# K and V with 32 adjacent keys of two kv-heads per partition, and staging in one tile

## The chip, the cores and the metric

The kernel runs on one core of a Trainium2 chip. The metric is the time of the device in microseconds for one execution; before the change it is 284.9 us, the median of three runs (283.17 to 286.01). A core has a matrix engine (PE, with its weight loads as PEld), a vector engine (DVE), a scalar engine (ACT), GpSimd (POOL) and SyncE (SP). ACT, SP and POOL issue transfers; all transfers run on the core's 16 DMA engines.

## The reference

A decode step of a block with attention over a sliding window and a gated FFN in parallel, forward and backward:

```python
def _A_ref(x, k_cache, v_cache, wq, wo):
    B, Sq, D = x.shape                    # 4, 1, 512
    Hq, Dh = 32, 128
    Hkv, Sk = k_cache.shape[1], k_cache.shape[2]   # 8, 4096
    W = min(4096, max(256, Sk // 4))      # 1024
    rep = Hq // Hkv
    q = (lambda x, *d: x.transpose(*d))((x @ wq).reshape(B, Sq, Hq, Dh), 0, 2, 1, 3)
    k = jnp.repeat(k_cache[:, :, Sk - W:, :], rep, axis=1)
    v = jnp.repeat(v_cache[:, :, Sk - W:, :], rep, axis=1)
    scores = jnp.einsum("bhqd,bhkd->bhqk", q, k) * (Dh ** -0.5)
    p = _softmax(scores, axis=-1)
    o = jnp.einsum("bhqk,bhkd->bhqd", p, v)
    return (lambda x, *d: x.transpose(*d))(o, 0, 2, 1, 3).reshape(B, Sq, Hq * Dh) @ wo
def _B_ref(x, w_gate, w_up, w_down):
    return (_gelu(x @ w_gate) * (x @ w_up)) @ w_down
xn = _layernorm(x, axis=-1)
return x + _A_ref(xn, ...) + _B_ref(xn, ...)
```

The results are this output and the gradients with respect to x, both caches and the five weights, all in bf16. The gradients of the caches have the full shape (4, 8, 4096, 128); outside the window of 1024 keys they are zero, so three quarters of each is a store of zeros.

## The kernel before, in words

There are B = 4 batches, G = 8 kv-heads with rep = 4 query heads each (Q = 32 query heads), J = 8, and the 128 partitions are used as four quadrants of 32 (`quad`).

The FFN comes first. Its weights, then wq, wo and the first K go out on SP's queue; the FFN's weight gradients are evicted from PSUM into staging tiles (`stg_tile`, line 101) and stored by `result` (line 112) on POOL's queue. The staging tiles are [128, 4096] bf16, 8 KB per partition, in rotation over four buffers.

The attention runs over the batches. `load_kv` (line 216) loads K (tiles ka and kb in turn) or V (tile va) of a batch as two transfers of 1 MB, each four kv-heads. Partition m holds 8 adjacent keys (m*8 to m*8+7) of all 8 heads, so a row of a transfer is 8 keys of one head, 2 KB. The DRAM side is written `"g (m j) d -> m g (j d)"`: 128 partitions outermost, then four heads. V of batch b+1 is loaded after the output matmuls of batch b, K of batch b+2 after the dq matmuls of batch b, all but the first K on POOL's queue.

`scores` (line 471) turns the tile with four DVE transposes of 32x32 blocks of bf16 pairs (`t32`), and multiplies with the block-diagonal query tiles bd, which `refill` (line 462) builds on POOL by eight copies per operand and batch. PE's column group c is here the head pair c, and the rows of a quadrant are four key chunks times 8 query heads. `softmax` (509) and `softmax_d` (536) work on [128, 256]. `turned` (496) transposes P or dS through PE into pT and evicts it with one cast of 256 columns. `odq` (567) multiplies pT with V or K. `spread` (487) and `dvdk` (550) form the gradients of V and K: 8 groups of PE results, evicted by `evac` (line 82, it chooses ACT or DVE by a running account of their load) into two staging tiles, which go out as two stores of 1 MB with rows of 2 KB.

The zeros are stores of 1.5 MB from one tile ztile, issued on SP's queue by `zeros` (line 236). Each waits for the zero store two (late in the kernel three) before it, and for an instruction that the caller names: after the loads the first of a group waits until that load has landed. The instruction order of SP's queue is written by hand; the other engines' is the scheduler's, in which the loads of K and V have high priority.

The weight gradients dwo and dwq end the kernel: eight stores of 1 MB with rows of 8 KB, on POOL's queue.

Of the kernel before, what the change touches and what calls it, by code (L numbers as in the profile page):

```python
# [9 lines left out]
ALU = mybir.AluOpType  # L10
AX = mybir.AxisListType
FP32 = mybir.dt.float32
BF16 = mybir.dt.bfloat16
# [5 lines left out]
def kernel(  # L19
# [54 lines left out]
    stage = ctx.enter_context(tc.tile_pool(name="stage", bufs=4, reuse_waits="tile"))  # L74
# [26 lines left out]
    def stg_tile():  # L101
        return stage.tile([P, 4096], BF16, name="stg", tag="stg")
# [46 lines left out]
    def mask(name, n, in_):  # L149
        t_ = const.tile([P, n], FP32, name=name)  # L150
        nc.vector.reduce_sum(out=t_[:], in_=in_, axis=AX.X)
        return t_
# [7 lines left out]
    omt = const.tile([P, NQ, 2], FP32, name="omt")  # L160
    TT(out=omt[:], in0=gmask[:].rearrange("p (c g) -> p c g", g=2), in1=bm[:].unsqueeze(2).broadcast_to([P, NQ, 2]),
       op=ALU.mult)
    om = mask("om", 2, omt[:].rearrange("p c g -> p g c"))
    oms = const.tile([P, 2], FP32, name="oms")
    TS(out=oms[:], in0=om[:], scalar1=scale, scalar2=None, op0=ALU.mult)
    gmask_b = const.tile([P, G], BF16, name="gmask_b")
    nc.vector.tensor_copy(out=gmask_b[:], in_=gmask[:])
    rs2 = const.tile([P, NQ, 4, 8], FP32, name="rs2")
    for c in range(NQ):
        TS(out=rs2[:, c], in0=m8[:].unsqueeze(1).broadcast_to([P, 4, 8]), scalar1=bm[:, c:c + 1], scalar2=None,  # L170
           op0=ALU.mult)
    rs2_f = rs2[:].rearrange("p c a r -> p (c a r)")
    selp = const.tile([P, 4, NQ, 8], BF16, name="selp")
    for a in range(4):
        TS(out=selp[:, a], in0=rs2[:, :, 0, :], scalar1=amask[:, a:a + 1], scalar2=None, op0=ALU.mult)
# [40 lines left out]
    def load_kv(b, k, pool, tag, eng, **kw):  # L216
        d_, src = ((k_t, A_k_cache), (v_t, A_v_cache))[k]
        tl = pool.tile([P, G, J, Dh], BF16, name=tag, tag=tag)
        for hf in range(2):
            hs = slice(hf * G // 2, (hf + 1) * G // 2)  # L220
            with tc.high_priority():
                d = eng.dma_start(out=tl[:, hs].rearrange("p g j d -> p g (j d)"),  # L222
                                  in_=src[b, hs, K0:Sk, :].rearrange("g (m j) d -> m g (j d)", j=J), **kw)
        d_[b] = tl
        return d
# [149 lines left out]
    with tc.tile_pool(name="mid", bufs=1, reuse_waits="tile") as mid:  # L375
# [4 lines left out]
        with tc.tile_pool(name="att", bufs=1, reuse_waits="tile") as att:  # L380
# [7 lines left out]
            for k in range(2):  # L388
                bd.append([])
                for u in range(2):  # L390
                    t_ = att.tile([P, DPB, NQ, 2, 2, Q], BF16, name=f"bd{k}{u}")
                    nc.gpsimd.memset(t_[:], 0.0)
                    bd[k].append(t_)
# [8 lines left out]
            for h in range(Hq):  # L402
                for c in range(C):
# [3 lines left out]
            qs2 = qsc[:, 512:1024].rearrange("p (b c a r) -> p b c a r", b=B, c=NQ, a=4)  # L407
            nc.scalar.activation(out=qs, in_=q_ps[:].rearrange("p h b -> p b h").unsqueeze(2).broadcast_to([P, B, NQ, Hq]),
                                 func=ACT.Copy, scale=scale)
            nc.vector.tensor_copy(out=qs2, in_=qs[:, :, 0, :].rearrange("p b (c r) -> p b c r", c=NQ).unsqueeze(3)  # L410
                                  .broadcast_to([P, B, NQ, 4, 8]))

            def spread_rows(k, get):

                ps = bank("r_ps", "x", (P, B, Dh))
                get(ps, 0)
                rb = scratch()[:].bitcast(BF16)[:, 0:512]
                nc.scalar.copy(out=rb, in_=ps[:].rearrange("p b d -> p (b d)"))
                t32(D3[k][:], pairs(rb), 256)
                ps = bank("r_ps", "x", (P, B, Dh))  # L420
                get(ps, 1)
                nc.scalar.activation(out=rows[k][:, :, 0, :], in_=ps[:], func=ACT.Copy, scale=g2m[:, 0:1])
                TS(out=rows[k][:, :, 1, :], in0=ps[:], scalar1=g2m[:, 1:2], scalar2=None, op0=ALU.mult)

            def get_q(ps, u):
                for b in range(B):
                    l_ = qs[:, b].rearrange("p a h -> p (a h)") if u == 0 else qs2[:, b].rearrange("p c a r -> p (c a r)")
                    mm(ps[:, b, :], l_, ident[:])
# [13 lines left out]
            for u in range(2):  # L442
# [5 lines left out]
            hsel2 = dsc[:, 640:768].rearrange("p (c a r) -> p c a r", c=NQ, a=4)  # L448
            nc.vector.tensor_copy(out=hsel, in_=hm[:].unsqueeze(1).broadcast_to([P, NQ, Q]))
            nc.vector.tensor_copy(out=hsel2, in_=hm[:].rearrange("p (c r) -> p c r", c=NQ).unsqueeze(2)  # L450
                                  .broadcast_to([P, NQ, 4, 8]))
# [4 lines left out]
            def get_d(ps, u):  # L456
                l_ = dsc[:, 512:640] if u == 0 else dsc[:, 640:768]
                mm(ps[:].rearrange("p b d -> p (b d)"), l_, dM.rearrange("p b e k -> p (b e k)"))
# [3 lines left out]
            def refill(k, b):  # L462

                src = D3[k][:].bitcast(BF16).rearrange("p b e (c g i r) -> p b g e c r i", c=NQ, g=2, r=2)
                t_ = bd[k][b % 2]
                for a, q in enumerate(quad):
                    for g2 in range(2):
                        o_ = a * 8 + g2 * 4
                        nc.gpsimd.tensor_copy(out=t_[q, :, :, g2, :, o_:o_ + 4], in_=src[q, b, g2])

            def scores(k, b):

                t_ = bd[k][b % 2]
                ps = bank("sc_ps", ("S", "dP")[k], (P, NJ))
                src = pairs((k_t, v_t)[k][b][:])
                for g2 in range(2):
                    for e in range(2):
                        sc = scratch()
                        t32(sc[:].rearrange("p (c j m) -> p c j m", c=NQ, j=J), src[:, g2:G:2, :, e * Q:(e + 1) * Q], 1024)
                        sb = sc[:].bitcast(BF16).rearrange("p (c n r) -> p c r n", c=NQ, r=2)  # L480
                        for r in range(2):
                            for c, q in enumerate(quad):
                                mm(ps[q, :], t_[:, e, c, g2, r, :], sb[:, c, r, :], g2 == 0 and e == 0 and r == 0,
                                   g2 == 1 and e == 1 and r == 1, (0, Q * c))
                return ps[:]
# [10 lines left out]
            def turned(src, k):  # L496

                ps = bank("pT_ps", "x", (P, J, Q))
                for j in range(J):
                    for a, q in enumerate(quad):  # L500
                        mm(ps[q, j, :], src[:, j * Q:(j + 1) * Q], selp[:, a].rearrange("p c r -> p (c r)"), pos=(0, Q * a))
                pT = att.tile([P, J, Q], BF16, name="pT", tag=f"pT{k}")
                evac(pT[:], ps[:], NJ)
                return pT
# [4 lines left out]
            def softmax(S):  # L509
# [4 lines left out]
                mx = small("mx", (1, NQ, 8))  # L514
                nc.vector.reduce_max(out=mx[:], in_=mT_ps[:].rearrange("o (c a r) -> o c r a", c=NQ, a=4), axis=AX.X)
                mx4 = small("mx4", (1, NQ, 4, 8))
                TS(out=mx4[:], in0=mx[:].unsqueeze(2).broadcast_to([1, NQ, 4, 8]), scalar1=-1.0, scalar2=None, op0=ALU.mult)
                nm_ps = bank("nm_ps", "x", (P, 1))
                mm(nm_ps[:], mx4[:].rearrange("o c a r -> o (c a r)"), one_f[:])
# [6 lines left out]
                mm(es_ps[:], rs2_f, es[:])  # L526
# [9 lines left out]
            def softmax_d(P_f, dP):  # L536
# [5 lines left out]
                mm(gs_ps[:], rs2_f, gs[:])  # L542
# [7 lines left out]
            def dvdk(k, b, sp, r_):  # L550

                og = (out_3, out_2)[k]
                stg = [stg_tile() for _ in range(2)]
                sv = [s_[:].rearrange("p (g j d) -> p j g d", g=4, j=J) for s_ in stg]
                for j in range(0, J, 2):
                    ps = [bank("kv_ps", "w", (P, 2, 2, Dh)) for _ in range(NQ)]
                    for u in range(2):
                        for c, q in enumerate(quad):
                            mm(ps[c][:, u].rearrange("p g d -> p (g d)"), sp[q, j + u].rearrange("p a m -> p (a m)"),
                               r_[q, b].rearrange("p g d -> p (g d)"), pos=(Q * c, 0))  # L560
                    for c in range(NQ):
                        evac(sv[c // 2][:, j:j + 2, (c % 2) * 2:(c % 2) * 2 + 2, :], ps[c][:], 512)
                for hf in range(2):
                    result(og[b, hf * 4:(hf + 1) * 4, K0:Sk, :].rearrange("g (m j) d -> m g (j d)", j=J),
                           stg[hf][:].rearrange("p (g e) -> p g e", g=4))

            def odq(k, b, pT):
# [3 lines left out]
                for j in range(J):  # L571
                    for c, q in enumerate(quad):
                        mm(ps[q].rearrange("p g d -> p (g d)"), pT[:, j, :], src[:, 2 * c:2 * c + 2, j, :],
                           j == 0, j == J - 1, (0, Q * c))
                mk = (om, oms)[k]
# [190 lines left out]
```

## Time and profile before

| | |
|---|---|
| median of three runs | 284.9 us |
| the profiled execution | 284.82 us |
| its span | 283.0 us |
| PE, DVE, ACT, POOL busy | 66%, 58%, 44%, 21% |
| moved | 112.21 MB, 396 GB/s over the span |
| SP's queue (q1) and POOL's queue (q0), share of 16 DMA engines | 57.0% and 40.8% |
| transfers of 1 MB for K and V | 16 loads, 16 stores |
| zero stores | 32 of 1.5 MB |

The span is the time from the first to the last instruction that the profiler saw; the execution's time has about 1.8 us more around it. A DMA packet is one contiguous piece that one of the 16 DMA engines moves; the share of a queue is the time of its packets over the span of 16 engines. Releasers are written with an arrow: "A <- B" is A waiting for B.

### The profile page before, as it was taken

How to read it: one execution, taken by the hardware profiler on the slowest of the kernel's cores; microseconds unless marked ns; L12 is line 12 of the kernel's file. 1: busy time of each engine (PE TensorE's matmuls, PEld its weight loads, DVE VectorE, ACT ScalarE, POOL GpSimd, SP SyncE). 2: the span in 40 equal slices, each digit the busy share in tenths (PEclk: the TensorE clock that was granted, in tenths of full speed). 3: DMA queues.
4: the chain of work that ended last, by engine and by line, in shares of the span. 5: the costliest groups of instructions: out<-in, count | busy, mean ns of one | idle time of the engine just before them, and what ended most of it. 6: DMA issues, size and time to landing. Idle time of an engine off the chain costs nothing.

```text
span 283.0 us, 4400 instructions
## 1 busy us (share of the span) xinstructions
PE 187.6 (66%) x1731; PEld 76.8 (27%) x1733; DVE 165.0 (58%) x309; ACT 124.4 (44%) x245; POOL 60.3 (21%) x135
## 2 busy tenths in 40 slices
PE   0225989859544899759976663923357998944870
PEld 0102344233111543234331341311034232510210
DVE  4779674898798533635257254055496104396970
ACT  2032774740010469744725420802432767454870
POOL 8500000169075313120040060200020020201110
PEclk9999965556955555755555555555555555685555
DMA  6999989999999999999999999999999999999995
GB/s 217 430 446 435 432 317 420 424 430 396 392 428 406 383 357 425 328 365 411 421 419 414 408 427 405 396 422 421 429 382 423 413 410 403 399 415 396 391 397 223
DMA packets 16883, 112.21 MB, mean 396 GB/s; under 512 B 1368, under 2 KB 1632, under 8 KB 11104
## 3 DMA queue, kind: packets, MB, share of 16 engines
q1 hardware_dynamic: 6544, 66.46, 57.0%
q0 software_dynamic: 10176, 45.35, 40.8%
q8 instruction: 13, 0.21, 0.3%
q10 hardware_dynamic: 144, 0.13, 0.2%
q14 instruction: 6, 0.05, 0.0%
HBM read 30.93 MB, written 81.01 MB: 396 GB/s over the span
## 4 chain that ended last, share of the span: by engine, by line
DMA 30%; issue 14%; PE 13%; DVE 9%; ACT 3%; POOL 2%; POOLq 0%; ACTq 0%; DVEq 0%
DMA out_dram<-stg 30%; DVE scr L93 4%; PE kv_ps L117 4%; PE od_ps L117 3%; PE sc_ps L117 2%; PE dwq_ps L117 2%; ACT stg L88 2%; DVE stg L89 1%; POOL out_dram L106 1%; PE ok_ps L117 1%; PE es_ps L117 1%; DVE spr L492 1%; DVE dqs L593 1%; ACT E_f L524 1%; PE nm_ps L117 1%
## 5 line engine op out<-in xcount | busy, mean ns | idle before, releaser
L88 ACT CAST stg<-kv_ps 128x512 bf16<-128x512 f32 x118 | 63.6, 606 | 52.2 <-DMA out_dram<-stg 26.3
L106 POOL DMA_DIRECT2D out_dram<-stg x30 | 19.7, 659 | 150.0 <-ACT stg L88 94.7
L117 PE MATMUL sc_ps<-scr,bd 128*32 128x256 bf16 x256 | 24.2, 396 | 15.2 <-DVE scr L93 15.2
L117 PE MATMUL kv_ps<-qm,spr 32*128 32x256 bf16 x128 | 24.8, 385 | 13.0 <-ACT stg L88 12.5
L117 PE MATMUL kv_ps<-dm,spr 32*128 32x256 bf16 x128 | 28.9, 399 | 6.6 <-ACT stg L88 4.9
L93 DVE STREAM_TRANSPOSE scr<-va 128x1024 uint32<-128x1024 uint32 x16 | 18.9, 1219 | 12.9 <-DMA va<-in_A_v_cache_dram 12.8
L117 PEld LDWEIGHTS <-spr 32*128 32x128 bf16 x256 | 12.4, 102 | 46.4 <-issue 42.1
L89 DVE CAST stg<-kv_ps 128x512 bf16<-128x512 f32 x10 | 6.6, 683 | 17.0 <-PE kv_ps L117 11.0
L117 PEld LDWEIGHTS <-bd 128*32 128x32 bf16 x256 | 8.1, 107 | 29.1 <-issue 28.5
L88 ACT CAST stg<-dwg_ps 128x448 bf16<-128x448 f32 x26 | 12.7, 554 | 6.4 <-PE dwg_ps L117 5.5
L88 ACT CAST stg<-dwo_ps 128x512 bf16<-128x512 f32 x18 | 10.0, 588 | 11.4 <-PE dwo_ps L117 10.1
L117 PE MATMUL dwo_ps<-dy_b,oSP 32*128 32x512 bf16 x32 | 9.0, 508 | 7.5 <-ACT stg L88 6.2
L93 DVE STREAM_TRANSPOSE scr<-ka 128x1024 uint32<-128x1024 uint32 x8 | 9.6, 1228 | 5.2 <-DMA ka<-in_A_k_cache_dram 3.1
L222 POOL DMA_DIRECT2D va<-in_A_v_cache_dram x8 | 6.0, 757 | 27.3 <-PE od_ps L117 25.8
L93 DVE STREAM_TRANSPOSE scr<-kb 128x1024 uint32<-128x1024 uint32 x8 | 9.8, 1232 | 3.5 <-DMA kb<-in_A_k_cache_dram 2.9
L117 PE MATMUL do_ps<-scr,dyBD 128*128 128x512 bf16 x31 | 10.1, 459 | 2.4 <-DVE scr L93 2.1
L578 DVE SCALAR_TENSOR_TENSOR odt<-od_ps,oms,odt 128x128 f32<-128x128 f32 x4 | 1.4, 340 | 17.0 <-ACT odt L577 17.0
L117 PE MATMUL dwq_ps<-dqSP,xn_b 32*128 32x512 bf16 x32 | 10.7, 586 | 0.9 <-ACT stg L88 0.3
L89 DVE CAST stg<-dwq_ps 128x512 bf16<-128x512 f32 x15 | 9.9, 689 | 1.6 <-PE dwq_ps L117 1.4
L89 DVE CAST stg<-dwo_ps 128x512 bf16<-128x512 f32 x14 | 9.2, 680 | 2.7 <-PE dwo_ps L117 2.7
L117 PEld LDWEIGHTS <-pT 128*32 128x32 bf16 x256 | 9.2, 140 | 5.2 <-ACT pT L88 2.3
L88 ACT CAST stg<-dwq_ps 128x512 bf16<-128x512 f32 x17 | 9.7, 586 | 1.4 <-PE dwq_ps L117 0.7
(196 smaller groups left out, 321.3 us busy)
## 6 DMA issues: line engine op xcount, KB each, us to landing
out_dram<-ztile SPq DMA_DIRECT2D x32, 1536.0 KB, 12.1
out_dram<-stg POOLq DMA_DIRECT2D x24, 1024.0 KB, 13.7
va<-in_A_v_cache_dram POOLq DMA_DIRECT2D x8, 1024.0 KB, 17.6
out_dram<-stg POOLq DMA_DIRECT2D x6, 896.0 KB, 10.2
wq_sb<-in_A_wq_dram SPq DMA_DIRECT2D x1, 4096.0 KB, 25.6
wo_sb<-in_A_wo_dram SPq DMA_DIRECT2D x1, 4096.0 KB, 36.7
kb<-in_A_k_cache_dram POOLq DMA_DIRECT2D x4, 1024.0 KB, 19.4
ka<-in_A_k_cache_dram SPq DMA_DIRECT2D x2, 1024.0 KB, 44.3
```

The lines of the kernel that those rows point to most:

```text
L88: return nc.scalar.copy(out=out, in_=in_)
L89: return nc.vector.tensor_copy(out=out, in_=in_)
L93: nc.vector.transpose(out=out, in_=in_)
L106: d = eng.dma_start(out=out, in_=in_, **kw)
L117: nc.tensor.matmul(out, lhsT=lhsT, rhs=rhs, start=first, stop=last, **kw)
L222: d = eng.dma_start(out=tl[:, hs].rearrange("p g j d -> p g (j d)"), in_=src[b, hs, K0:Sk, :].rearrange("g (m j) d -> m g (j d)", j=J), **kw)
L492: TS(out=sp[:, :, a, :], in0=src[:].rearrange("p (j m) -> p j m", j=J), scalar1=amask[:, a:a + 1], scalar2=None, op0=ALU.mult)
L524: nc.scalar.activation(out=E_f[:], in_=S, func=ACT.Exp, bias=negm[:, 0:1], scale=1.0, accum_out=es[:])
L578: done = STT(out=t_[:], in0=ps[:, 1, :], scalar=mk[:, 1:2], in1=t_[:], op0=ALU.mult, op1=ALU.add)
L593: nc.vector.tensor_copy(out=dqs[q, :, :, :, a * B + b], in_=d3v[q])
```

## The change

K and V are laid out anew. A partition now holds 32 adjacent keys of two kv-heads: quadrant q holds the head pair q (heads 2q and 2q+1), and partition m in it the keys m*32 to m*32+31. A transfer is one head of each pair (g2), so a row is 32 keys of one head, 8 KB; the DRAM side is `"q (m j) d -> q m (j d)"`. On PE the column groups are now the key quarters, and rows of a quadrant are all 32 query heads. So the masks, the block-diagonal tiles (`refill` is now two products with a mask instead of eight copies, and the memsets go), the order of heads in the softmax and the sums over partitions change with it; one form of the rows (`spread_rows`) serves where there were two. `turned` masks pT to its head pair while it evicts it: the cast of 256 columns on ACT or DVE becomes a DVE product of 1024 columns. The four staging tiles become one tile of four slots, because an eviction of `dvdk` now writes into both of its slots; `stg_tile(2)` gives an aligned pair.

```diff
-    stage = ctx.enter_context(tc.tile_pool(name="stage", bufs=4, reuse_waits="tile"))
+    stage = ctx.enter_context(tc.tile_pool(name="stage", bufs=1))
...
-    def stg_tile():
-        return stage.tile([P, 4096], BF16, name="stg", tag="stg")
+    stg_all = stage.tile([P, 4, 4096], BF16, name="stg")
+    stg_next = [0]
+
+    def stg_tile(n=1):
+
+        k = stg_next[0] = -(-stg_next[0] // n) * n
+        stg_next[0] += n
+        return stg_all[:, k % 4] if n == 1 else stg_all[:, k % 4:k % 4 + n]
...
-    rs2 = const.tile([P, NQ, 4, 8], FP32, name="rs2")
-    for c in range(NQ):
-        TS(out=rs2[:, c], in0=m8[:].unsqueeze(1).broadcast_to([P, 4, 8]), scalar1=bm[:, c:c + 1], scalar2=None,
-           op0=ALU.mult)
-    rs2_f = rs2[:].rearrange("p c a r -> p (c a r)")
-    selp = const.tile([P, 4, NQ, 8], BF16, name="selp")
-    for a in range(4):
-        TS(out=selp[:, a], in0=rs2[:, :, 0, :], scalar1=amask[:, a:a + 1], scalar2=None, op0=ALU.mult)
+    selp = const.tile([P, NQ, 4, 8], BF16, name="selp")
+    for c in range(4):
+        for a in range(NQ):
+            TS(out=selp[:, c, a, :], in0=m8[:], scalar1=amask[:, c:c + 1], scalar2=bm[:, a:a + 1], op0=ALU.mult,
+               op1=ALU.mult)
...
-        tl = pool.tile([P, G, J, Dh], BF16, name=tag, tag=tag)
-        for hf in range(2):
-            hs = slice(hf * G // 2, (hf + 1) * G // 2)
+        tl = pool.tile([P, 2, Q, Dh], BF16, name=tag, tag=tag)
+        for g2 in range(2):
             with tc.high_priority():
-                d = eng.dma_start(out=tl[:, hs].rearrange("p g j d -> p g (j d)"),
-                                  in_=src[b, hs, K0:Sk, :].rearrange("g (m j) d -> m g (j d)", j=J), **kw)
+                d = eng.dma_start(out=tl[:, g2].rearrange("p j d -> p (j d)"),
+                                  in_=src[b, g2::2, K0:Sk, :].rearrange("q (m j) d -> q m (j d)", j=Q), **kw)
...
-                t_ = bd[k][b % 2]
-                for a, q in enumerate(quad):
-                    for g2 in range(2):
-                        o_ = a * 8 + g2 * 4
-                        nc.gpsimd.tensor_copy(out=t_[q, :, :, g2, :, o_:o_ + 4], in_=src[q, b, g2])
+                for g2 in range(2):
+                    nc.gpsimd.tensor_tensor(out=bd[k][b % 2][:, g2], in0=src[:, b],
+                                            in1=hmask[:, g2].unsqueeze(1).unsqueeze(1).broadcast_to([P, DPB, 2, Q]),
+                                            op=ALU.mult)
...
-                pT = att.tile([P, J, Q], BF16, name="pT", tag=f"pT{k}")
-                evac(pT[:], ps[:], NJ)
+                load["dve"] += 1200
+                pT = att.tile([P, J, NQ, NQ, 8], BF16, name="pT", tag=f"pT{k}")
+                TT(out=pT[:].rearrange("p j a c r -> p (j a) c r"),
+                   in0=ps[:].rearrange("p j (a r) -> p (j a) r", a=NQ).unsqueeze(2).broadcast_to([P, J * NQ, NQ, 8]),
+                   in1=bm[:].unsqueeze(1).unsqueeze(3).broadcast_to([P, J * NQ, NQ, 8]), op=ALU.mult)
...
-                stg = [stg_tile() for _ in range(2)]
-                sv = [s_[:].rearrange("p (g j d) -> p j g d", g=4, j=J) for s_ in stg]
+                stg = stg_tile(2)
+                sv = stg.rearrange("p g (j d) -> p j g d", j=Q)
...
-                    for c in range(NQ):
-                        evac(sv[c // 2][:, j:j + 2, (c % 2) * 2:(c % 2) * 2 + 2, :], ps[c][:], 512)
-                for hf in range(2):
-                    result(og[b, hf * 4:(hf + 1) * 4, K0:Sk, :].rearrange("g (m j) d -> m g (j d)", j=J),
-                           stg[hf][:].rearrange("p (g e) -> p g e", g=4))
+                    for a in range(NQ):
+                        evac(sv[:, J * a + j:J * a + j + 2], ps[a][:], 512)
+                for g2 in range(2):
+                    result(og[b, g2::2, K0:Sk, :].rearrange("q (m j) d -> q m (j d)", j=Q), stg[:, g2])
```

## The prediction

> **What bounds the kernel now.** I read first the engines' shares, the forty slices, the DMA queues and the DMA issues of the page.
>
> ```profile
> span 283.0 us, 4400 instructions
> ...
> PE 187.6 (66%) x1731; PEld 76.8 (27%) x1733; DVE 165.0 (58%) x309; ACT 124.4 (44%) x245; POOL 60.3 (21%) x135
> ...
> DMA  6999989999999999999999999999999999999995
> ...
> DMA packets 16883, 112.21 MB, mean 396 GB/s; under 512 B 1368, under 2 KB 1632, under 8 KB 11104
> ...
> q1 hardware_dynamic: 6544, 66.46, 57.0%
> q0 software_dynamic: 10176, 45.35, 40.8%
> ...
> out_dram<-ztile SPq DMA_DIRECT2D x32, 1536.0 KB, 12.1
> out_dram<-stg POOLq DMA_DIRECT2D x24, 1024.0 KB, 13.7
> va<-in_A_v_cache_dram POOLq DMA_DIRECT2D x8, 1024.0 KB, 17.6
> ```
>
> No compute engine is above 66%, while the 16 DMA engines are full in nearly every slice. The two large queues fill 57.0 + 40.8 = 97.8% of 16 engines' span, 276.8 of 283.0 us; about 5 us (first load, last landing) are not theirs. So the kernel is a DMA schedule: what a change does to the packets is worth its full price, and what it does to an engine is worth nothing while that engine keeps the queues fed. The sum below is made on the profiled execution (284.82 us, 1.8 above its span), which agrees with the median of the three runs, 284.9. Their spread (283.17 to 286.01) means that a difference under about 1% can't be told from none.
>
> Next, what the queues wait for (SP's waits) and when POOL issues (timeline of POOL).
>
> ```profile
> SPq L106 <- DMA out_dram<-ztile: 127.1, 21, 14.5
> ...
> SPq L106 <- DMA va<-in_A_v_cache_dram: 23.2, 4, 9.2
> SPq L106 <- DMA ka<-in_A_k_cache_dram: 13.3, 1, 13.3
> ```
>
> ```profile
> 162.63 1.50 POOL L222 DMA_DIRECT2D va<-in_A_v_cache_dram  x2 [16.20 <-PE od_ps L117]
> 164.12 1.50 POOL L106 DMA_DIRECT2D out_dram<-stg  x2
> ...
> 182.12 1.50 POOL L106 DMA_DIRECT2D out_dram<-stg  x2 [14.66 <-ACT stg L88]
> 206.23 0.75 POOL L106 DMA_DIRECT2D out_dram<-stg  x1 [22.61 <-DVE stg L89]
> 207.48 0.75 POOL L106 DMA_DIRECT2D out_dram<-stg  x1 [0.50 <-ACT stg L88]
> 228.84 0.75 POOL L106 DMA_DIRECT2D out_dram<-stg  x1 [20.61 <-ACT stg L88]
> ```
>
> The zero stores (SP's queue) are the filler: they wait for the zero store two or three before them and, in groups, for a load to land. A zero store is complete only when its slowest DMA engine is. So if some DMA engines fall behind, the zeros are held back for all of them.
>
> **The change, part by part.** (1) *Longer rows.* K and V are 16 MB loaded and 16 MB stored, 32 transfers of 1 MB (16 loads, 16 stores; 30 on POOL's queue, two on SP's). In the trace's packet records POOL's 30 are 7680 packets of 4096 B, mean 169.4 ns, SP's two 1024 packets of 2048 B, mean 85.4 ns. Now all have rows of 8 KB, as the dwo and dwq stores have: 1024 packets of 8192 B, mean 318.2 ns. The DMA time per engine, if spread over all 16: before (7680 x 169.4 + 1024 x 85.4) / 16 = 86.8 us, after 4096 x 318.2 / 16 = 81.5 us, a gain of 5.3 us. With the medians (160, 84, 315 ns) it is only 1.5 us: the long packets are hardly faster per byte, and the mean of the short ones contains crowded stretches.
>
> (2) *How many DMA engines carry one transfer.* Before, the DRAM side ran over m (128) first, then the heads; both sides of each K/V transfer counted 128. Now the DRAM side is "q m (j d)": 4 head pairs outermost, 32 rows in each, against 128 partitions in SBUF. No large transfer of before has a 4 outermost. The nearest rows are the two small result stores (out_b, dx_b), four rows each. The 1368 packets under 512 B show how they are spread: there are 85 large or 128-partition transfers (44 by POOL, 40 by SP, 1 by ACT) and these two, and 85 x 16 + 2 x 4 = 1368. These tiny packets are one per participating engine, so a transfer with 4 outermost took four engines. The ends for the new transfers are therefore 16 (their SBUF side still counts 128) and 4; I take 4, from the only rows with that outer count. Then one 1 MB transfer is 32 packets of 8 KB on each of four engines, 32 x 318.2 ns = 10.2 us, and leaves twelve engines to others. What matters is how the 32 transfers fall on the engines. SP's two (the first K) come from the queue that sent the small stores; I put both on the same four: 20.4 us there. POOL's 30 can't be dealt evenly to four groups: 8, 8, 7, 7 if taken in turn. The ends are wide, for the trace does not show which engines a transfer takes: dealt perfectly nothing is lost, and all on one group would be 30 x 10.2 + 20.4 = 326 us there, a time of 284.8 - 86.8 + 326 = 524. I take turns, by the row above: POOL's 44 transfers all took every engine alike, so nothing marks four of them out for it, and I give the far end no more than 2 in 100. With turns the fullest group carries 8 x 10.2 + 20.4 = 101.9 us against 86.8 before: **+15.1 us**. If that group gets seven, +4.9 us.
>
> [...]
>
> (3) *What the concentration does to the others.* The load and store pairs alternate on POOL (va and stores at 162.6 and 164.1), and a pair fills eight engines, so mostly a load pair on one half stands beside a store pair on the other. Where a pair has no partner (stores at 182.1 and 228.8), the half without it runs ahead and waits for the zeros to complete: at most the pair's own 10.2 us each. At 182 the loads of 162.6 are still being worked off on the other half, so I take nothing; at 228.8 the next pair follows 12 us later, and I take half, **+5.1 us**. Bounds 0 and 20.4.
>
> (4) *One staging tile.* Each eviction now writes both stores' slots, so a first eviction waits for both earlier stores instead of one; the second is issued 0.75 us after the first (1.50 for two), 8 x 0.75 = 6 us of ACT waiting at most. Behind the waiting ACT stand its exp and odt work and, through the four PSUM banks, PE's kv_ps matmuls. The gap from slot 9 to 10 is a free slot. Cover: the zeros and loads in flight; taken as 0.
>
> (5) *The turned P and dS.* ACT's cast pT 128x256 (402 ns) becomes a DVE product of 1024 columns. Between DVE's 128x512 from PSUM (L423, 0.71 us) and twice that: 1.42 us at most, so up to +1.0 us x 8 = 8 us in the batches' serial chains, and -0.40 x 8 on ACT. Off the DMA queues: 0; if that cover is gone, up to 8.
>
> (6) *Small edits.* Refills: 64 POOL copies of 229 ns become 16 products of 128 columns (POOL's nearest row is 0.97 us for 1024, so 0.1 to 0.5 each): some 7 us less POOL; four bd memsets (0.97 each) fall away. Second row spread: 4 + 1 matmuls (307 to 460 ns) and two DVE copies fewer, some 2 us between 68 and 80 us. Masks: sixteen selp products at 236 ns for four, less four rs2 at 299 and three small ones, +1.4 us of DVE before xn_b; the weights that follow land later than that. Scores, odq and dvdk keep their counts and shapes. All stand beside full DMA queues: 0. POOL's issue order stays, an issue of 128 rows took 0.53 us against 0.75: 0.
>
> Sum: 284.8 + 15.1 + 5.1 = **305.0 us**.
>
> **The rivals.** *All sixteen engines* (the other side, faster): if POOL spreads by partitions, part 2 falls away and only part 1 stays: 284.8 - 5.3 = 279.5, or 283.3 by medians. For it: every POOL transfer so far has 16 participants and SBUF still counts 128. Against: the 4 is outermost now, as in the two small stores. It decides as soon as a 1 MB load alone on the queues lands in far less than 10 us.
> *Collapse of the cover* (slower): the zeros are gated by five later load pairs (SP waited 23.2 + 13.3 us on such loads already). If each leaves eight engines idle for half of its 10.2 us, 25.5 us, and both lone store pairs cost their full 10.2, with part 5's 8 us uncovered: 284.8 + 15.1 + 20.4 + 25.5 + 8 = 353.8, and all above 328 is this case. One staging tile that serializes its halves would end there too: a store landing (13.7) on each of seven gradient pairs, +96 at most. Against: before, load and store pairs overlapped.
> *Even enough* (no large effect): the group with SP's loads gets seven, and longer rows and quicker landings on free engines offset the rest: 283 to 291.
>
> **How the numbers follow.** Four engines with the fullest group as the bound 0.62: its own range 290 (seven shares, no idling: 284.8 + 4.9) to 328 (both lone pairs in full, part 5 uncovered: 284.8 + 15.1 + 20.4 + 8). All sixteen 0.17, collapse 0.11, even enough 0.10. The range reaches into the first rival, 280 to 328. Faster by over 1%: most of the first rival, 0.15; within 1%: the rest of it and half of "even enough", 0.08; slower 0.77.
>
> **What would show it.** Right: packets of 8192 B on both queues; the count under 512 B falls by 2 x 12 on SP's queue; the DMA row of the slices shows 7 and 8 where it had 9; a K or V load takes at least 10.2 us; SP waits longer for zeros. Wrong: DMA row full to the end and a shorter span (sixteen engines), or DMA clearly idle while ACT and PE wait for stg (the staging tile).

## The result, and the profile after

The changed kernel takes 407.2 us (median of four, 403.99 to 410.08) against 284.4 us before: 1.43 times as long, 95% interval 1.412 to 1.443. The direction was forecast; the size was not, and the time lies far above the range of 280 to 328. Here and below a median and the range beside it hold all runs of a kernel, while a ratio to before, with its interval, leaves out runs that took over 1.5% longer than the kernel's fastest.

The parts of the changed kernel's page that answer to those shown of before:

```profile
span 402.2 us, 4365 instructions
...
PE 189.5 (47%) x1728; PEld 73.3 (18%) x1728; DVE 169.8 (42%) x314; ACT 126.5 (31%) x247; POOL 48.4 (12%) x83
...
DMA  7999958998599799999999589979999689999577
GB/s 273 438 441 370 419 229 201 152 186 302 219 429 309 186 143 194 312 317 261 294 319 350 184 266 256 331 234 254 222 238 330 263 224 293 268 283 358 213 309 292
DMA packets 23772, 112.26 MB, mean 279 GB/s; under 512 B 12865, under 2 KB 13129, under 8 KB 13897
...
q0 software_dynamic: 17856, 45.40, 45.9%
q1 hardware_dynamic: 5752, 66.46, 42.4%
...
out_dram<-ztile SPq DMA_DIRECT2D x32, 1536.0 KB, 18.4
out_dram<-stg POOLq DMA_DIRECT2D x24, 1024.0 KB, 35.0
va<-in_A_v_cache_dram POOLq DMA_DIRECT2D x8, 1024.0 KB, 34.2
```

The engines are hardly busier than before (PE 187.6 us then and 189.5 now, DVE 165.0 and 169.8), so the 119 us of span are waiting, and the transfers come first in question. Two things must be read together. The DMA row has holes (5, 6, 7 and 8 where there were nines). And where it is full, the GB/s row beneath it is not: 152 or 143 GB/s under a 9. A stretch of the kernel before with full queues moved 367 GB/s (stretch, length, busy time of PE, PEld, DVE, ACT and POOL, granted PE clock, DMA share, GB/s):

```profile
97.00:125.00 28.00, 24.05 (x256) 10.85 (x255) 11.52 (x29) 19.74 (x41) 6.17 (x11) 0.56 0.99 367
```

The same view of the changed kernel shows few engines at work from 56 to 60 us, full but slow ones from 138 to 152, and a hole from 224 to 230:

```profile
56.00:60.00 4.00, 3.85 (x26) 0.98 (x23) 2.27 (x7) 4.00 (x10) 0.53 (x1) 0.50 0.29 120
...
138.00:152.00 14.00, 0.00 (x0) 0.00 (x0) 0.00 (x0) 0.00 (x0) 0.00 (x0) 0.50 1.03 143
224.00:230.00 6.00, 1.12 (x8) 0.34 (x7) 0.00 (x0) 1.76 (x4) 0.00 (x0) 0.50 0.42 150
```

From 138 to 152 us all 16 DMA engines are at work on four loads (V issued at 121.6 us, K at 134.9) and two stores of the changed form and move 143 GB/s, while no compute engine does anything. The 8 KB packets that start there take 937 ns on average: a busy DMA engine is here one whose packet takes about three times the 318 ns of the weight-gradient stores before. From 56 to 60 us between four and five engines are busy (0.29 of 16), by the packet records about half of them with SP's two first K loads and half with the end of a weight-gradient store. The waits say who paid; before:

```profile
ACT stg L88 <- DMA out_dram<-stg: 28.2, 7, 7.0
...
DVE scr L93 <- DMA va<-in_A_v_cache_dram: 12.8, 3, 6.4
```

and after:

```profile
SPq L112 <- DMA out_dram<-ztile: 233.6, 25, 49.9
...
DVE scr L93 <- DMA va<-in_A_v_cache_dram: 85.0, 5, 25.8
ACT stg L88 <- DMA out_dram<-stg: 75.1, 10, 24.4
```

DVE waited 12.8 us for V before and 85.0 us now; ACT waited 28.2 us for staging slots and 75.1 now; SP waited 127.1 us for earlier zero stores and 233.6 now.

The trace's packet records turn this into a sum, in us per DMA engine (the packets' total time over 16; idle is the span less that):

| | before | after | difference |
|---|---|---|---|
| K/V packets (32 transfers of 1 MB) | 86.8 | 149.4 | +62.6 |
| zero stores | 120.9 | 129.6 | +8.7 |
| packets of 4 and 8 bytes | 0.8 | 7.5 | +6.8 |
| other transfers | 69.9 | 70.0 | +0.1 |
| idle | 4.7 | 45.7 | +41.0 |
| span | 283.0 | 402.2 | +119.2 |

In this account more than half of the loss is K/V packets that take longer: POOL's 3840 packets of 8 KB took 597 ns on average, not the 318 ns of the dwo and dwq stores. A third is idle DMA time. The account alone does not say which of the rows causes the others.

### The profile page after: what moved, and what is told of

Read it like the earlier page. It is cut to its first block, busy times and chain, and to the rows that moved or that the text cites. A ratio compares the mean times of both kernels' runs of the same rounds, so it can differ in the third digit from the quotient of the medians.

```text
span 402.2 us, 4365 instructions
## 1 busy us (share of the span) xinstructions
PE 189.5 (47%) x1728; PEld 73.3 (18%) x1728; DVE 169.8 (42%) x314; ACT 126.5 (31%) x247; POOL 48.4 (12%) x83
## 3 DMA queue, kind: packets, MB, share of 16 engines
q1 hardware_dynamic: 5752, 66.46, 42.4%
## 4 chain that ended last, share of the span: by engine, by line
DMA 62%; PE 17%; DVE 8%; ACT 5%; issue 2%; another core or an unknown queue 2%; POOL 1%; POOLq 0%; ACTq 0%; DVEq 0%
DMA out_dram<-stg 42%; DMA va<-in_A_v_cache_dram 19%; PE kv_ps L123 4%; ACT stg L88 4%; PE od_ps L123 3%; DVE scr L93 2%; PE dwo_ps L123 2%; PE dwg_ps L123 1%; PE dwq_ps L123 1%; DVE pT L493 1%; PE da_ps L123 1%; PE h_ps L123 1%; DVE selp L178 1%; DMA x_b<-in_A_x_dram 1%
## 5 line engine op out<-in xcount | busy, mean ns | idle before, releaser
L88 ACT CAST stg<-kv_ps 128x512 bf16<-128x512 f32 x125 | 67.3, 600 | 71.5 <-DMA out_dram<-stg 36.8
L123 PE MATMUL sc_ps<-scr,bd 128*32 128x256 bf16 x256 | 22.4, 403 | 75.1 <-DVE scr L93 74.5
L123 PE MATMUL kv_ps<-dm,spr 32*128 32x256 bf16 x128 | 27.5, 401 | 17.3 <-ACT stg L88 17.3
L123 PE MATMUL kv_ps<-qm,spr 32*128 32x256 bf16 x128 | 26.7, 399 | 10.4 <-ACT stg L88 10.4
L123 PE MATMUL dwo_ps<-dy_b,oSP 32*128 32x512 bf16 x32 | 10.6, 592 | 34.5 <-ACT stg L88 34.5
L88 ACT CAST stg<-dwo_ps 128x512 bf16<-128x512 f32 x21 | 11.4, 594 | 37.0 <-DMA out_dram<-stg 33.0
L516 ACT ACTIVATE E_f<-sc_ps,negm 128x256 f32<-128x256 f32 x4 | 2.0, 490 | 59.7 <-DVE negm L513 59.7
L493 DVE TENSOR_TENSOR pT<-pT_ps,bm 128x1024 bf16<-128x1024 f32 x8 | 9.7, 1206 | 23.1 <-PE pT_ps L123 23.1
L123 PE MATMUL od_ps<-ka,pT 128*32 128x256 bf16 x64 | 5.5, 407 | 20.2 <-DVE pT L493 20.2
L89 DVE CAST stg<-dwo_ps 128x512 bf16<-128x512 f32 x11 | 7.1, 680 | 10.7 <-issue 7.5
## 6 DMA issues: line engine op xcount, KB each, us to landing
va<-in_A_v_cache_dram POOLq DMA_DIRECT2D x8, 1024.0 KB, 34.2
```

What stands on the lines that cost most here:

```text
L88: return nc.scalar.copy(out=out, in_=in_)
L89: return nc.vector.tensor_copy(out=out, in_=in_)
L123: nc.tensor.matmul(out, lhsT=lhsT, rhs=rhs, start=first, stop=last, **kw)
L493: TT(out=pT[:].rearrange("p j a c r -> p (j a) c r"), in0=ps[:].rearrange("p j (a r) -> p (j a) r", a=NQ).unsqueeze(2).broadcast_to([P, J ...
L516: nc.scalar.activation(out=E_f[:], in_=S, func=ACT.Exp, bias=negm[:, 0:1], scale=1.0, accum_out=es[:])
```

## The experiments

Four questions: is the form of the transfers the whole loss, which property of the form makes the packets slow, what does the narrow spread itself cost, and what do the other edits cost. In several of these kernels K and V hold other keys or heads, as the expectations say; then only their times count.

### The form alone

The kernel before with the changed transfers (p2), and the changed kernel with flat transfers (p3).

```diff
 # p2: before.py
-                d = eng.dma_start(out=tl[:, hs].rearrange("p g j d -> p g (j d)"),
-                                  in_=src[b, hs, K0:Sk, :].rearrange("g (m j) d -> m g (j d)", j=J), **kw)
+                d = eng.dma_start(out=tl[:, hs].rearrange("p g j d -> p (g j d)"),
+                                  in_=src[b, hf::2, K0:Sk, :].rearrange("q (m j) d -> q m (j d)", j=Q), **kw)
 ...
 # p3: after.py
-                                  in_=src[b, g2::2, K0:Sk, :].rearrange("q (m j) d -> q m (j d)", j=Q), **kw)
+                                  in_=src[b, 4 * g2].rearrange("(m j) d -> m (j d)", j=Q), **kw)
```

(The stores are edited in the same way.)

> The kernel before with one thing of the change: the K and V loads and the stores of their gradients go out in the changed form (4 groups of 32 rows of 8 KB) into and out of the same tiles, so that keys and heads lie in wrong places; layout, masks, evictions and the four staging tiles stay. Theory 1 (the form of the transfers is the whole loss): 390 to 410 us. Theory 2 (the single staging tile or the longer chain of turned carries much of it): under 350.

> The changed kernel with each K/V transfer as 128 contiguous rows of 8 KB (loads read other keys, stores go to a whole head, the zeros to the other six heads of the batch, as many bytes as before). Theory 1 (the form of the transfers is the whole loss): 278 to 285 us, the gain of the longer packets that the prediction gave (5.3 us, or 1.5 by medians). Theory 2 (staging tile or chain): over 320.

Measured: p2 388.4 us (386.9 to 397.9), ratio to before 1.359 (1.348 to 1.370). p3 283.3 us (281.7 to 284.7), ratio 0.991 (0.987 to 0.995). From the page of p3:

```profile
DMA  6999999999999987999999999999999999999973
...
DMA packets 12275, 112.21 MB, mean 401 GB/s; under 512 B 1368, under 2 KB 1632, under 8 KB 2400
...
q1 hardware_dynamic: 5776, 66.46, 56.9%
q0 software_dynamic: 6336, 45.35, 39.0%
```

Rows of 8 KB spread over all engines, with every other edit of the change in place, fill the queues again and are 0.9% faster than before. The form of the transfers carries 103 of some 122 us by itself, so theory 1 holds in the main, though p2 lies just under its 390 us; the other edits cost nothing that shows while the queues are full. Longer rows and the other edits together are worth 2 to 3 us, between the 1.5 and 5.3 that the two averages had given for the rows; no run has the rows alone.

### Why a packet is slow

The probe runs transfers by themselves, one stage after another (p1). Its core, with the forms as functions of the tensor, the batch and the half:

```diff
+    for n in (1, 2):
+        for f, s_ in ((ld2k, rows2k), (ld, flat), (ld, four), (ld, near(4)), (ld, near(2)), (ld, near(8)), (ld, rows8k)):
+            fence()
+            for i in range(n):
+                f(i, s_(V, i // 2, i % 2))
```

> Transfers by themselves, all else of the computation left out: stages of loads and then of stores of 1 MB on POOL's queue, one stage after the landing of the one before, with one, two or four transfers in flight. Forms: 2 KB rows as before (128 outermost); 128 rows of 8 KB, contiguous in DRAM; the changed form, 4 groups of 32 rows, the groups 2 MB apart; groups of 32 rows (4 of them), 64 rows (2) and 16 rows (8) with only 8 KB between the groups; 32 rows outermost with four places 2 MB apart in each. [...] Theory B (DRAM: streams 2 MB apart hit the same place of the memory): the changed form is slow, every form with near groups about 310. Theory C (only the number of engines): every packet 310, a single transfer lands after 10 us in the changed form and 20 us with two groups.

From its packet records, loads of 1 MB each:

| form | in flight | us | GB/s | median ns of an 8 KB packet |
|---|---|---|---|---|
| 128 contiguous rows | 1 | 3.6 | 296 | 309 |
| changed form (4 groups of 32, 2 MB apart) | 1 | 15.6 | 67 | 437 |
| 4 groups of 32, 8 KB between | 1 | 14.5 | 72 | 361 |
| 2 groups of 64 | 1 | 21.3 | 49 | 309 |
| 8 groups of 16 | 1 | 8.8 | 119 | 534 |
| 32 rows outermost, four places 2 MB apart | 1 | 3.0 | 355 | 309 |
| changed form | 2 | 19.7 | 107 | 544 |
| 2 groups of 64 | 2 | 22.5 | 93 | 309 |
| 128 contiguous rows | 4 | 10.9 | 385 | 309 |
| changed form | 4 | 44.1 | 95 | 1213 |

The windows of the last two (and of four stores, flat and then changed), here with DVE and POOL as the only engines:

```profile
225.10:236.00 10.90, 0.00 (x0) 0.86 (x2) 1.00 0.94 383
238.40:282.50 44.10, 0.00 (x0) 1.25 (x2) 1.00 0.91 95
360.40:370.70 10.30, 0.00 (x0) 1.04 (x2) 1.00 1.00 407
373.00:400.50 27.50, 0.00 (x0) 1.43 (x3) 1.00 0.70 152
```

With four in flight nearly all 16 engines work (share 0.91), so POOL does deal its transfers to different engines; but four such loads take four times as long as flat ones, at 1213 ns per packet, nearly four times 309. The distance in DRAM is not the cause: groups 264 KB apart are as slow as groups 2 MB apart (14.5 and 15.6 us), and 32 rows outermost with places 2 MB apart run at full rate (3.0 us, 355 GB/s). Theory B falls. Theory C falls as well, since packets are slow (437 ns alone, 544 with two in flight, 1213 with four). Two groups of 64 keep the median of 309 ns, with the same bytes and as large a packet; what differs is how many groups there are and which partitions each of them has. Two probes varied the partition step alone:

```diff
-            nc.gpsimd.dma_start(out=t[:, slot], in_=src, single_packet=True)
+            nc.gpsimd.dma_start(out=t[0:32 * step:step, 0], in_=rows32(V, rep, 0), single_packet=True)  # r1
+            nc.gpsimd.dma_start(out=t[0:64 * step:step, 0], in_=rows64(V, rep, 0), single_packet=True)  # s1
```

> Transfers by themselves (the rest of the computation is left out): 32 rows of 8 KB in 4 groups of 8, one transfer at a time on POOL's queue, three times loads and three times stores, with the 32 SBUF partitions 1, 2 or 4 apart; same DRAM rows, same number of engines, same packets. [...]

Measured (three times each): stores 2.9 to 3.0 us at step 1, 4.0 to 4.1 at step 2, 4.5 at step 4. Loads 3.5 to 3.6, 3.7 to 4.3 and 3.4 to 3.6. The stores change with the partitions; the loads are slower at step 2 only, and not at step 4. With eight packets per group the start (first load packets of up to 1454 ns) is a large part of the whole. This probe left the loads open; the next one has 32 packets per group.

> Transfers by themselves (the rest of the computation is left out): 64 rows of 8 KB in 2 groups of 32, so two engines with 32 packets each, the 64 SBUF partitions 1 or 2 apart; three times as loads, three times as stores, then loads with two and four transfers in flight. DRAM rows, packets and engines are the same for both steps. [...] Theory G (DRAM, or engines that hinder each other whatever the partitions): both steps alike, in the loads above all, where the probe with three steps did not part them.

Measured: loads at step 1 14.3, 15.6 and 13.4 us, at step 2 11.1, 10.9 and 11.6; stores 13.0, 12.8 and 13.6 against 11.4 each time. Step 1 is slower than step 2 every time, in the loads too, so theory G falls. With four loads in flight, step 1 and then step 2:

```profile
215.80:255.70 39.90, 0.00 (x0) 1.21 (x2) 1.00 0.46 53
258.70:273.30 14.60, 0.00 (x0) 1.14 (x2) 1.00 0.44 144
```

The same DRAM rows, the same packets, the same share of engines (0.46 and 0.44), and 53 or 144 GB/s by the partitions alone. With the two groups of 32 on partitions 0 to 31 and 32 to 63 the mean packet takes 1090 ns; with the groups on the even partitions of 0 to 62 and of 64 to 126 it takes 358. The changed form has its four groups on partitions 0 to 31, 32 to 63, 64 to 95 and 96 to 127, so neighbouring groups lie 32 apart as in step 1. That its packets (437 to 1213 ns) are slow for the same reason is my estimate from these runs.

That the partitions decide is shown; by what means they do is not. And that several transfers use the same partitions is not enough: at step 2 with four in flight, and in two loads of two groups of 64, they do, and their packets take 358 and 334 ns on average. Why these get by, and groups 32 apart do not, no run here settles.

### Narrow spread or slow packets

Two forms that exchange one for the other: quarters (p4, 32 partitions outermost, 512 KB each) and two groups of 64 (q3).

```diff
 # p4
-        for g2 in range(2):
+        for a, q in enumerate(quad):
             with tc.high_priority():
-                d = eng.dma_start(out=tl[:, g2].rearrange("p j d -> p (j d)"),
-                                  in_=src[b, g2::2, K0:Sk, :].rearrange("q (m j) d -> q m (j d)", j=Q), **kw)
+                d = eng.dma_start(out=tl[q].rearrange("p g j d -> p g (j d)"),
+                                  in_=src[b, 2 * a:2 * a + 2, K0:Sk, :].rearrange("g (m j) d -> m g (j d)", j=Q), **kw)
 # q3
+                                  in_=src[b, 0:2, g2 * 2048:(g2 + 1) * 2048, :].rearrange("h (m j) d -> h m (j d)", j=Q), **kw)
```

> The changed kernel with each pair of transfers cut by quadrants: four transfers of 512 KB, 32 partitions outermost on both sides, two rows of 8 KB in each. [...] Theory C (only the number of engines mattered): 280 to 287.

> The changed kernel with each K/V transfer as 2 groups of 64 rows of 8 KB (loads read other keys, stores go to two heads, zeros to the other six): two engines per transfer, which alone took 309 ns per packet, 21 us in all. [...] Theory C (the narrow spread itself: long landings and zeros that wait for the slowest engine): slower than the changed kernel, 410 to 460.

Measured: p4 338.7 us, ratio 1.189 (1.179 to 1.199). q3 448.9 us, ratio 1.572 (1.556 to 1.588). By the packet records (the mean of POOL's first 3840 packets of 8 KB, which are those of K and V; idle DMA time):

| kernel | engines per transfer | ns per packet | idle us | time us |
|---|---|---|---|---|
| flat (p3) | 16 | 315 | 10.1 | 283.3 |
| quarters (p4) | 16 (estimate) | 472 | 20.0 | 338.7 |
| changed kernel | 4 | 597 | 45.7 | 407.2 |
| two groups (q3) | 2 | 383 | 131.1 | 448.9 |

The engines per transfer are read from SP's tiny packets. SP's queue has 5776, 5752 and 5748 packets flat, changed and in two groups, 5128 of them larger; this leaves 648, 624 and 620, so 16, 4 and 2 for each of SP's two K loads. For the quarters the 16 is an estimate from the probe's form with 32 rows outermost: 128 packets of 309 ns in 3.0 us are 13 at a time.

So there are two losses. Quarters, by that estimate, keep the engines on each transfer and still lose 19% with packets of 472 ns, where theory C gave 280 to 287 us. Two groups bring the packets most of the way back to 315 ns and still lose more: a load of 1 MB in two groups lasts 21.3 us alone in the probe, idle DMA time rises to 131.1 us, and the tiny packets on POOL's queue grow to 27584 (15.1 us per engine against 0.4 flat). I had held 330 to 390 us open for q3 because of its shorter packets; that failed. Theory C's 410 to 460 came, and the narrow spread by itself is the worse of the two there.

### Loads, stores and the zeros

Only the loads in the changed form (q1), only the stores (q2), the others flat.

```diff
 # q1: stores
-                    result(og[b, g2::2, K0:Sk, :].rearrange("q (m j) d -> q m (j d)", j=Q), stg[:, g2])
+                    result(og[b, g2].rearrange("(m j) d -> m (j d)", j=Q), stg[:, g2])
 # q2: loads
-                                  in_=src[b, g2::2, K0:Sk, :].rearrange("q (m j) d -> q m (j d)", j=Q), **kw)
+                                  in_=src[b, 4 * g2].rearrange("(m j) d -> m (j d)", j=Q), **kw)
```

> The changed kernel with only the loads in the changed form (4 groups of 32 rows); the gradient stores go as 128 contiguous rows to whole heads and the zeros to the other heads. [...] Theory D (the loss comes through the staging slots, which the stores hold): under 320.

> The changed kernel with only the gradient stores in the changed form; the loads read 128 contiguous rows of 8 KB (other keys). [...] Theory D (staging slots): over 360.

Measured: q1 361.1 us (352.0 to 364.9), q2 384.2 us (375.4 to 386.4), before 286.2 beside them. By the fastest run of each, loads alone cost 66 us and stores alone 89, by the medians 75 and 98, both together some 122: they overlap. The fastest q2 is slower than the slowest q1, so the order is safe. I had expected more from the loads, as they were slower in the probe (95 GB/s with four in flight, the stores 152); theory D was right on the stores (over 360 us) and wrong on the loads (under 320). From the profiled q2 (385.4 us):

```profile
ACT stg L88 <- DMA out_dram<-stg: 133.7, 8, 34.7
...
PE kv_ps L123 <- ACT stg L88: 94.7, 6, 32.0
```

In the kernel with only the stores changed, ACT waits 133.7 us for slots and PE 94.7 us behind ACT, the chain that part 4 of the prediction named.

Then the zeros were let go (r2), with the kernel before as control (r3).

```diff
-            if len(zdone) >= deep:
-                behind(z.ins, zdone[-deep].ins)
-            if after is not None:
-                behind(z.ins, after.ins)
+            if len(zdone) >= 6:
+                behind(z.ins, zdone[-6].ins)
```

> The changed kernel with the zero stores let go: each waits only for the sixth one before it, for no load or other instruction. If the zeros' gates made the idle DMA time (46 of 402 us), it shrinks to 20 or less and the time falls to 370 to 390; if the idle time comes from the loads and stores themselves (compute waits for them and then has nothing to send), the time stays at 400 or rises, since the zeros take the engines from the loads.

> The control: the kernel before with the zero stores let go in the same way. Its DMA engines are full as it is, so the zeros only go earlier and the loads later: 285 to 300 us by either theory.

Measured: r2 429.7 us (425.6 to 438.0), ratio 1.489 (1.483 to 1.495), idle 81.1 us; r3 327.1 us, ratio 1.145 (1.141 to 1.149), idle 47.2 us. The control missed what I expected by any theory. The DMA rows of r2 and then of the control:

```profile
DMA  7999999999999999899999644396386364356577
...
DMA  6999999999999999999999999993992602472796
```

The control is full to the 27th slice, then empty in places: the zeros went early and were missing as filler at the end. The gates of `zeros` are worth 41 us to the kernel before. In r2 the idle time moves in the same way: 10.0 us up to the last zero packet (254 us) and 71.2 us behind it, against 38.4 and 7.4 in the changed kernel, whose last zero packet ends at 377 us. So the gates do keep zeros out of holes that they could fill, but without them the time is longer. Whether other gates would cover more is open.

### The staging

p2 with the staging of the change (one tile of four slots, each eviction into both slots of its pair).

```diff
-                stg = [stg_tile() for _ in range(2)]
+                stg = stg_tile(2)
 ...
-                        evac(sv[c // 2][:, j:j + 2, (c % 2) * 2:(c % 2) * 2 + 2, :], ps[c][:], 512)
+                        evac(sv[:, J * c + j:J * c + j + 2], ps[c][:], 512)
```

> The kernel before with the transfers of the changed form and in addition the staging of the change: one tile of four slots, each eviction writes into both slots of its pair (keys and heads lie in wrong places). The changed kernel took 407 us, this one without the new staging 388. Theory E (staging makes the difference): 400 to 410. Theory F (the longer chain of the DVE product in turned and the other edits make it, or the order of POOL's issues): 385 to 392.

Measured: 402.3 us, ratio 1.405 (1.393 to 1.416), against 1.359 (1.348 to 1.370) without it. The staging costs 13 to 14 us where stores land late; flat, it costs nothing that p3 shows. What remains to the changed kernel (1.428, 1.412 to 1.443) overlaps with this interval: the longer `turned` and the rest are not shown to cost anything.

## Why the prediction was wrong

**Part 1, longer rows: right as far as shown.** 5.3 or 1.5 us of gain were given; the flat kernel, with the other edits in it, shows 0.9%, 2 to 3 us.

**Part 2, four engines per transfer: right in the count, wrong in the price, and this is the step that failed.** SP's tiny packets fell by 2 x 12 (648 to 624), and no more than four of its K packets ran at a time, but for 0.2 us. POOL dealt its transfers to different engines (share 0.91 with four in flight). But "32 packets of 8 KB on each of four engines, 32 x 318.2 ns = 10.2 us" took the packet time from stores that spread over all engines. In the changed form the packet measured 597 ns on average; that the partitions alone can do this, s1 shows (1090 or 358 ns for the same rows). 3840 packets with 278 ns more make 67 us per engine, where the term for the transfers had only unevenness, +15.1. Whether the fullest group carried that unevenness can't be read, since the packet records don't name the engine. Also missing: 12224 four-byte packets on POOL's queue instead of 704, 384 more per transfer, which is 12 x 32, as if each of the twelve unused engines got one for every packet of a used one (+6.8 us per engine). So the reading that tiny packets count the engines of a transfer held on SP's queue and not on POOL's.

**Part 3, idle time: far too small, the second term that failed.** +5.1 us with bounds 0 and 20.4; measured +41.0. The reasoning looked only at zeros that wait for the slowest engine, and took each pair's 10.2 us as the most that could be lost. That wait grew: of the 16 completions that the trace records for a zero store, the last came 2.8 us after the first before (median of the 24 stores that it gives a landing, at most 4.8) and 10.4 us in the changed kernel (16 stores, at most 23.3). Compute waits as well: loads land after 34.2 us instead of 17.6, stores after 35.0 instead of 13.7 (medians), and DVE waits 72 us longer for V and ACT 47 us longer for slots, with little new to issue meanwhile. How the 41 us divide between these waits and the gates of the zeros is not measured.

**Part 4, staging: too small.** At most 6 us were given, 0 taken; 13 to 14 us once the stores land late. The place, ACT and behind it PE, was right.

**Parts 5 and 6: right with cover, not settled without.** Flat, they cost nothing. The pT product took 1206 ns, within the bound of 1420. The sixteen selp products (3.1 us) came after xn_b, not before it, and ahead of the first FFN matmuls; the queues were full by then.

**The rivals.** "All sixteen engines" was not what the chip did, but as an experiment it gave 283.3; that this is the very figure by medians is partly luck, since p3 has the other edits in it and runs from 281.7 to 284.7. "Collapse of the cover", 353.8, was the nearest case and had only 0.11. Its idle time (20.4 + 25.5 us) is near the 41.0 measured, but it put all of it down to gated zeros, and it had no slow packets. The range ended at 328 because every case priced the packet alike.

## What to carry to other kernels

Before a DMA is reshaped for longer rows, look at the outermost dimension of its DRAM side: here 1 MB by itself had about four packets at a time with 4 outermost (128 x 437 ns in 15.6 us), two with 2 (128 x 309 ns in 21.3 us) and 13 with 32 (128 x 309 ns in 3.0 us), an estimate from the probe's medians; and the partitions of the groups decided how long a packet took (1090 or 358 ns in s1). The same 8 KB rows from four places 2 MB apart, with 32 outermost, landed at 355 GB/s against 67; they then lie in other partitions, and no kernel was built on that. A packet's time from another transfer did not hold here when the spread changed (309 ns flat, 437 to 1213 in the changed form); give the price an upper end then (here two to four times 309 ns). In a profile read the DMA share and the GB/s together, since a share of 1.03 at 143 GB/s is not a full queue but a blocked one.

## What the runs showed of the hardware that I had not expected

Four loads of the changed form in flight (share of the 16 engines 0.91) moved 95 GB/s, flat ones 385. The partition step alone made 53 or 144 GB/s of the same four loads at the same share of engines (0.46 and 0.44). Rows of 2 KB left POOL's queue as packets of 4 KB at 160 ns (median of the kernel before), so that rows of 8 KB at 309 ns had little left to gain; a packet is then not always one contiguous piece, as it was introduced. Loads in two groups of 64 kept the median of 309 ns even with a second such transfer beside them.
